# Pooled-key attention with a mixture of adapters on one core: key loads in paced pieces, pooling of later batches on GpSimd, query casts per group, scores four chunks ahead

## The chip, the cores and the metric

The kernel runs on one core of one Trainium2 chip. The metric is device microseconds of a whole execution. Times are medians of repeated executions; the profile is one execution recorded by the hardware profiler, and its span is a little shorter than the device time of the same execution. The engines are PE (TensorE, matmul), PEld (its weight loads), DVE (VectorE), ACT (ScalarE), POOL (GpSimd) and SP (SyncE, which here only issues DMAs). SPq, ACTq and POOLq are the instruction sequencers of those engines.

## The reference

Shapes: `q` is (4, 12288, 128), `kv` is (4, 384, 32, 128), all fp32.

```python
# attention: keys and values are one 4x4 mean pool of kv, projected
kv_pool = kv.reshape(B, H//4, 4, W//4, 4, C).mean(axis=(2, 4))   # 768 keys per batch
k = v = kv_pool.reshape(B, -1, C) @ w_sr
a = softmax(q @ k.T / sqrt(C))
x = (a @ v).reshape(49152, 128)
# mixture of adapters: top 2 of 8 experts by x @ w_gate, softmax over the two
for expert e in the top two:  delta += w_e * (x @ A[e]) @ B[e]     # rank 16
return x + delta
```

## The kernel before

The work is cut into 96 chunks of 512 queries, 24 per batch. Four chunks make a group (`GC = 4`), for which the routing is done at once. The 768 pooled keys of a batch are six key chunks of 128. One pass of the main loop is called a slot. In a slot the kernel computes scores of chunk k, the attention product of chunk k - LA, the normalisation of chunk k - LA - 1, and, later, the adapters of an older chunk. Helpers `keep` and `mm` hold the instructions of each engine in program order.

The key load and its pooling on VectorE:

```python
def load_kv(b, engines):                       # one 6 MB tile for a batch, four DMAs
    t = prep.tile([P, HL, 4, WL * 4, C], FP32, tag="kvr", name="kvr")
    ...
# pool_step, five per third of a batch:
    keep(nc.vector.tensor_tensor(u, u, v, op=ALU.add))
```

The main loop (cut):

```python
LA = 2
for k in range(NCHUNK + LB + 2):
    ...
        if i == 0 and b + 1 < B:
            load_kv(b + 1, [nc.sync])            # 6 MB on the SP queue at once
            cast_q(b + 1, 0, NB // GC)           # q fp32 -> bf16, DRAM to DRAM, whole batch
            pending = prepare(b + 1, 3)
        if k % GC == 0:
            load_qT(k // GC + 2)                 # transposed load, SP queue, two groups ahead
        scores(k, 0)                             # PE sg, ACT exp
    normalize(kn); transposes(kx, kh); ...       # VectorE rinv, xn; PE tt_ps
    top(kn); route(...)                          # VectorE max8, POOL lgs copy, VectorE m, arg, mask, gw
    ...
    finish(kh)                                   # VectorE osb (4 buffers), SP store to out
    ...
    if i >= 3:
        for _ in range(2):
            if pending: pending.pop(0)()         # pooling adds, then key and value projections
```

Three kinds of transfer share the SP queue and pass through it in order: key loads, transposed query loads and output stores. The `lgs` copies, the issues of the query casts and, in the changed kernel, the pooling adds share the GpSimd instruction stream in order. Batches and their keys are counted from 0, as in the code: the keys of batch 2 arrive while batch 1 is computed.

The softmax here doesn't subtract the row's maximum and nothing guards it: scores larger than these inputs give would overflow.

## Time and profile before

| quantity | before | where it is read |
|---|---|---|
| device time, median of 4 runs | 610.21 us (609.62 to 611.39) | timed runs |
| PE busy | 405.8 us, 67% of the span | page, part 1 |
| first score matmul | 76.9 us | timeline of PE |
| steady pace | 3.91 us per chunk (four chunks 15.64) | starts of the normalisation |
| last score to end | 28.2 us (579.8 to 608.0) | timeline of PE |

The page of the kernel before, parts 1 and 2. Part 2 cuts the span in 40 slices, each digit a busy share in tenths; 15 us are one slice.

```profile
PE 405.8 (67%) x4436; PEld 304.1 (50%) x4507; DVE 385.8 (63%) x1045; ACT 289.9 (48%) x313; POOL 23.6 (4%) x107
...
PE   0000270778999920478899970087899999999974
...
DMA  8999099233144999933334699942314444442222
```

PE has no work for four slices at the start, and falls to 0 three times later (slices 7, 16 and 25 to 26), each time where the DMA row is at 9: new keys are arriving.

The waits of the kernel before (who, for what: us in total, times, longest).

```profile
PE acc L66 <- DVE xn L227: 105.9, 30, 31.6
DVE kvr L150 <- DMA kvr<-in_kv_dram: 78.1, 3, 29.3
...
DVE osb L310 <- DMA out_dram<-osb: 7.4, 2, 3.9
```

VectorE runs its instructions in the order of the program. Its first pooling add (`kvr`) of a batch waits for the keys, three times for 78.1 us in total, and everything that VectorE owes to PE waits behind it: PE stands for `xn` as long. The windows show one such stop against a steady stretch (us, then for each engine busy us and instructions, then clock, DMA share and GB/s).

```profile
220.00:240.00 20.00, 0.00 (x0) 0.00 (x0) 0.00 (x0) 0.61 (x1) 0.00 (x0) 0.54 1.03 203
...
480.00:500.00 20.00, 19.72 (x233) 14.90 (x234) 17.43 (x54) 15.74 (x18) 1.06 (x5) 1.00 0.37 94
```

In the first, PE and VectorE do nothing in 20 us while the DMA engines are full at 203 GB/s. In the second, PE is busy 19.72 of 20 us: it is the limit of the steady state. Three groups of the kernel before matter later (busy us, mean ns of one, then idle before).

```profile
L213 ACT ACTIVATE em<-sg 128x1024 f16<-128x1024 f32 x288 | 283.5, 1022 | 231.8 <-PE sg L66 163.7 <-PE d_ps L66 41.2 <-PE acc L66 18.5
...
L150 DVE TENSOR_TENSOR kvr<-kvr 128x1024 f32<-128x1024 f32 (+5 forms) x50 | 54.9, 1113 | 78.6 <-DMA kvr<-in_kv_dram 78.1
...
L265 DVE SCALAR_TENSOR_TENSOR gw<-th,mask 128x128 f32<-128x128 f32 x24 | 6.7, 281 | 0.3 <-ACT th L257 0.3
```

### The profile page before, as it was taken

Reading aid. Unit: us, or ns where it says so; the run is one execution under the profiler, and the core shown is the slowest. Engines: PE = TensorE matmul, PEld = TensorE weight load, DVE = VectorE, ACT = ScalarE, POOL = GpSimd, SP = SyncE. Lnnn points to the kernel's source line nnn. Section 1 sums busy time; section 2 is a strip of 40 time slices with the busy share of each in tenths; the row PEclk is TensorE's granted clock in tenths of the full one; section 3 lists DMA queues with packets and bytes.
Section 4 is the critical chain, followed back from the end, with each engine's and each line's share of the span. In section 5 each row is a group of like instructions: output and inputs, shape, how many; then the busy total and the mean of one; then the engine's idle time right before and its main releaser. Section 6 shows DMA issues by size and latency. Waiting matters only on the chain.

```text
span 608.0 us, 11014 instructions
## 1 busy us (share of the span) xinstructions
PE 405.8 (67%) x4436; PEld 304.1 (50%) x4507; DVE 385.8 (63%) x1045; ACT 289.9 (48%) x313; POOL 23.6 (4%) x107
## 2 busy tenths in 40 slices
PE   0000270778999920478899970087899999999974
PEld 0000140556777710356677750065677777777752
DVE  0002810798788810589788850288878888888884
ACT  0000080455677720146577760054567777777720
POOL 1000000000000000000000000000000000000000
PEclk9999996689999975589999995588999999999995
DMA  8999099233144999933334699942314444442222
GB/s 199 262 250 199 22 205 196 61 71 87 55 105 105 205 193 203 196 61 79 86 90 107 140 203 203 216 104 71 87 53 106 105 105 106 105 106 64 62 80 74
DMA packets 108995, 76.41 MB, mean 126 GB/s; under 512 B 53008, under 2 KB 102416, under 8 KB 108560
## 3 DMA queue, kind: packets, MB, share of 16 engines
q1 hardware_dynamic: 106208, 59.78, 43.3%
q0 software_dynamic: 464, 12.58, 9.9%
q10 hardware_dynamic: 2272, 3.35, 2.3%
q8 instruction: 35, 0.57, 0.4%
q14 instruction: 16, 0.13, 0.1%
HBM read 50.53 MB, written 37.75 MB: 145 GB/s over the span
## 4 chain that ended last, share of the span: by engine, by line
DVE 33%; PE 31%; DMA 26%; SPq 5%; issue 4%; ACT 0%; DVEq 0%; ACTq 0%
DMA kvr<-in_kv_dram 24%; PE acc L66 13%; DVE kvr L150 8%; PE sg L66 7%; DVE xn L227 7%; DVE tts L283 6%; SPq L95 5%; PE d_ps L66 4%; DVE hg L297 4%; PE tt_ps L66 3%; PE h_ps L66 2%; DMA b_f<-in_moe_B_dram 2%; DVE osb L310 2%; DVE rinv L225 2%; DVE gw L265 1%
## 5 line engine op out<-in xcount | busy, mean ns | idle before, releaser
L213 ACT ACTIVATE em<-sg 128x1024 f16<-128x1024 f32 x288 | 283.5, 1022 | 231.8 <-PE sg L66 163.7
L66 PE MATMUL acc<-vx,em 128*128 128x137 f16 x2304 | 181.5, 229 | 107.8 <-DVE xn L227 105.9
L66 PEld LDWEIGHTS <-em 128*128 128x128 f16 x2304 | 155.6, 101 | 140.7 <-DVE xn L227 136.0
L66 PE MATMUL sg<-qT,kfT 128*128 128x512 bf16 x505 | 158.6, 385 | 2.6 <-ACT em L213 2.3
L150 DVE TENSOR_TENSOR kvr<-kvr 128x1024 f32<-128x1024 f32 (+5 forms) x50 | 54.9, 1113 | 78.6 <-DMA kvr<-in_kv_dram 78.1
L310 DVE TENSOR_TENSOR osb<-d_ps,xn 128x512 f32<-128x512 f32 x96 | 66.2, 690 | 25.1 <-PE d_ps L66 17.8
L66 PEld LDWEIGHTS <-tts 128*128 128x128 bf16 x768 | 53.2, 101 | 45.7 <-DVE tts L283 22.9
L227 DVE TENSOR_TENSOR xn<-acc,rinv 128x544 f32<-128x544 f32 x96 | 69.5, 724 | 3.3
L297 DVE TENSOR_TENSOR hg<-h_ps,gw 128x512 bf16<-128x512 f32 x96 | 66.3, 691 | 5.4 <-PE h_ps L66 2.9
L283 DVE COPY tts<-tt_ps 128x1024 bf16<-128x1024 bf16 (+1 forms) x97 | 65.9, 680 | 2.6 <-PE tt_ps L66 2.6
L66 PEld LDWEIGHTS <-kfT 128*128 128x128 bf16 x576 | 46.7, 99 | 7.7 <-issue 5.4
L66 PE MATMUL d_ps<-b_bf,tts 128*128 128x128 bf16 x384 | 39.6, 228 | 6.3 <-DVE tts L283 4.1
L66 PEld LDWEIGHTS <-xn 128*128 128x128 bf16 x384 | 29.7, 98 | 28.0 <-issue 7.1
L66 PE MATMUL tt_ps<-id_bf,xn 128*128 128x128 bf16 x384 | 37.5, 221 | 7.1 <-DVE osb L310 5.9
L241 POOL COPY lgs<-xn 128x32 f32<-128x32 f32 x96 | 20.3, 211 | 563.9 <-DVE xn L227 563.9
L66 PE MATMUL h_ps<-a_bf,tts 128*128 128x128 bf16 x384 | 39.1, 227 | 1.5 <-issue 0.4
L66 PE MATMUL tt_ps<-id_bf,hg 128*128 128x128 bf16 x384 | 38.0, 222 | 2.0 <-DVE hg L297 2.0
L66 PE MATMUL wT_ps<-id_f,w_sr_sb 128*128 128x128 f32 x1 | 0.4, 448 | 56.9 <-DMA w_sr_sb<-in_w_sr_dram 56.9
L225 DVE RECIPROCAL rinv<-acc 128x4 f32<-128x4 f32 x96 | 17.1, 178 | 29.9 <-PE acc L66 29.7
L240 DVE MAX8 srt<-xn 128x8 f32<-128x8 f32 x384 | 34.7, 152 | 0.1
L120 DVE COPY wext<-w_sr_sb 128x128 f32<-128x128 f32 x1 | 0.2, 227 | 54.1 <-DMA w_sr_sb<-in_w_sr_dram 54.1
L66 PEld LDWEIGHTS wT_ps<-id_f,w_sr_sb 128*128 128x128 f32 x1 | 0.2, 183 | 56.9 <-issue 56.9
(81 smaller groups left out, 109.3 us busy)
## 6 DMA issues: line engine op xcount, KB each, us to landing
out_dram<-osb SPq DMA_DIRECT2D x96, 256.0 KB, 2.3
kvr<-in_kv_dram SPq DMA_DIRECT2D x14, 1536.0 KB, 31.8
kvr<-in_kv_dram ACTq DMA_DIRECT2D x2, 1536.0 KB, 49.7
qbf_0_174<-in_q_dram POOLq DMA_DIRECT2D x1, 3072.0 KB, 38.5
qbf_0_1807<-in_q_dram POOLq DMA_DIRECT2D x1, 3072.0 KB, 18.5
qbf_0_3695<-in_q_dram POOLq DMA_DIRECT2D x1, 3072.0 KB, 19.3
qbf_1_165<-in_q_dram POOLq DMA_DIRECT2D x1, 2560.0 KB, 22.9
qbf_0_98<-in_q_dram POOLq DMA_DIRECT2D x1, 512.0 KB, 10.0
```

The costliest lines, as they stand in the source:

```text
L66: return keep(nc.tensor.matmul(*a, **k))
L95: keep(engines[w % len(engines)].dma_start(t[32 * w:32 * w + 32].rearrange("p l r x c -> p l r (x c)"), src[w]))
L150: keep(nc.vector.tensor_tensor(u, u, v, op=ALU.add))
L213: keep(nc.scalar.activation(em[k][:, 2 * r:2 * r + 2], ps, AF.Exp, bias=0.0, scale=scale))
L225: keep(nc.vector.reciprocal(ri, acc[k][:, :, VC]))
L227: keep(nc.vector.tensor_tensor(x, acc[k][:, :, 0:VC], ri.unsqueeze(2).broadcast_to([P, S, VC]), op=ALU.mult))
L240: keep(nc.vector.max(srt[g][:, m, s], xn[k][:, s, C:VC]))
L241: keep(nc.gpsimd.tensor_copy(lgs[g][:, m], xn[k][:, :, C:VC]))
L265: keep(nc.vector.scalar_tensor_tensor(w, th, 1.0, mask, op0=ALU.add, op1=ALU.mult))
L283: keep(nc.vector.tensor_copy(sb[:, lo:hi], ps[:, lo:hi]))
L297: keep(nc.vector.tensor_tensor(hg[k].rearrange("p s (e r) -> p (s e) r", e=E), hp[k].rearrange("p s (e r) -> p (s e) r", e=E), gw[g][:, m ...
L310: keep(nc.vector.tensor_tensor(osb, dp[k], xn[k][:, :, 0:C], op=ALU.add))
```

## The change

The intent: start the matmuls while the first keys still arrive, keep the waiting for later keys off VectorE, and take the pooling work (54.9 us of VectorE) away from it for three of four batches. The diff, cut to its core:

```diff
-    qpool bufs=3, ppool bufs=3, xpool bufs=12                  # (shortened)
+    kvpool bufs=4, qpool bufs=4, ppool bufs=7, xpool bufs=9    # opool stays at 4
@@ start
-    load_kv(0, [nc.sync, nc.scalar])
-    cast_q(0, 0, 1)
+    cast_q(0)                                   # a cast is now one group, not a batch
+    for g in range(J):                          # six 1 MB pieces, each four DMAs
+        load_kv(0, g // WL, slice(4 * (g % WL), 4 * (g % WL) + 4), [nc.sync, nc.scalar])
+        if g == 2:
+            load_qT(0)
@@ first group
+    for h in range(3):                          # pool and project two key chunks,
+        for item in sums[10 * h:10 * h + 10] + rest[2 * h:2 * h + 2]:
+            item()
+        for k in range(LA):                     # then their scores for four query chunks
+            scores(k, h)
@@ scores
-    ... AF.Exp, bias=0.0, scale=scale)
+    ... AF.Exp, bias=shift, scale=scale)        # shift: a tile of -0.25
@@ main loop
-    LA = 2
+    LA = 4
-        load_kv(b + 1, [nc.sync]); cast_q(b + 1, 0, NB // GC); pending = prepare(b + 1, 3)
-        load_qT(k // GC + 2)
+            if g + 1 < B * NG and g + 1 not in qT:
+                load_qT(g + 1)                  # one group ahead
+            if g + 2 < B * NG and g + 2 not in q_bf:
+                cast_q(g + 2)
+            if i == 4:
+                sums, rest = prepare(b + 1, nc.gpsimd)
+            if i in (4, 5, 6):                  # 2 MB pieces, three slots in a row
+                load_kv(b + 1, i - 4, slice(0, 2 * 4), [nc.sync])
+            if i >= 8:                          # three pooling adds per slot
+                for _ in range(3):
+                    if sums: sums.pop(0)()
@@ end of a slot
+        if i >= 18 and rest:                    # projections of the next batch's keys
+            rest.pop(0)()
+            if len(rest) > NB - 1 - i:
+                rest.pop(0)()
@@ routing groups
+    sizes = [GC] * (NCHUNK // GC - 2) + [2, 2, 2, 1, 1]
```

## The prediction

> **What bounds it now.** Three regimes. (a) Start: the windows show no matmul work until 57 us; the timeline has the first score matmul at 76.9 us after 13 us of serial VectorE pooling. (b) Steady state (windows 460 to 580): PE busy 19.7 of every 20 us, 3.91 us per chunk (acc chain, 15.63 us per four chunks). (c) Batch changes: the chain of waits has "DMA kvr" at 24% of the span. VectorE's in-order pooling waits for the next keys, so everything stops, about 20 us at 87 to 107, 32 at 216 to 248 and 31 at 360 to 392 (waits: DVE kvr <- DMA 78.1 us in three waits). Then pooling (54.9 us over four batches) makes VectorE the limit, about 5.2 us per chunk for some ten chunks.
>
> **What the change does.**
> 1. Start: pooling per 1 MB piece and the scores of four chunks overlap the load; weights go first. From the DMA packets: keys 31 us of all engines, three casts about 3.2 us each, one transposed load 2.7. I expect keys to end near 46 us, first scores at 20 to 25, the main loop near 53. Saves about 25 us.
> 2. Pooling of batches 1 to 3 goes to GpSimd. The Trainium skill, "GPSIMD Engine Reference", section 3.1, has a two-input fp32 add at 4497 ns for 2048 elements; so I estimate 1.2 us for 128x512, 0.65 and 0.35 for the small ones, 28 us per batch, at most 3.7 us per chunk, just under 3.91. "SBUF — State Buffer", section "SBUF: two separate sides", lets GpSimd block VectorE only in two-SBUF-input or 2-port operations; the large VectorE ones here read PSUM (xn 724, osb 690, hg 691 ns should stay). VectorE then needs 3.4 us per chunk; PE bounds. Saves about 31 us.
> 3. The stalls: VectorE no longer waits for keys. But output stores and transposed query loads share the SP queue, first in first out, behind 6.3 MB of keys (30 us at 204 GB/s measured), plus casts, which take nearly all engines when active (packets). With four output buffers, stores behind the second and third key piece land late: I expect VectorE (osb <- DMA out_dram) or PE (sg <- DMA qT, now prefetched one group ahead, not two) to stall 10 to 20 us per batch, about 45 in all, instead of 84.
> 4. Tail: smaller last routing groups, about 5 to 8 us less than the 28 after the last score.
>
> **Sum.** 53 start + 92 iterations x 3.91 = 360, less 5 for the empty first ones, + 14 for key/value projections on PE + 20 tail = 442, if nothing stalls; + 45 = 487. I shade to 483, as the placement looks tuned against such stalls. Nearly all is on the critical path. Range 452 to 512; faster 0.98, same 0.01, slower 0.01.
>
> **What would show it.** Step 1: first sg before 27 us, PE dense from about 53. Step 2: POOL kvr groups near 1.2 us at 128x512, POOL busy about 105 us, no DVE kvr after 50 us. Step 3: the waits list "DVE kvr <- DMA" gone from batch changes; in its place one idle stretch of 10 to 20 us per batch around slots 8 to 12, ended by out_dram or qT.
>
> **What would make it wrong.** Stores not stuck behind keys (then 440 to 450); GpSimd adds at 1.7 us or more, so that its in-order lgs copies hold up routing (then above 500); VectorE lengthened by GpSimd; 2 KB key packets slower than 4 KB ones, delaying the start.

## The result and the profile after

| | median us | fast runs, lowest to highest | ratio to before, 95% interval |
|---|---|---|---|
| before | 610.21 | 609.62 to 611.39 | |
| after | 513.12 | 510.90 to 515.95 | 0.841 (0.836 to 0.846) |

A ratio, here and below, is the mean time of one kernel's fast runs over that of the other's fast runs of the same rounds, so it is not quite the ratio of the medians. The change is worth 16%. All outputs are right. The prediction had 483 us with a range that ended at 512; the measured median lies just above that range.

The page of the kernel after, parts 1 and 2; a slice is now 12.8 us.

```profile
PE 411.9 (80%) x4444; PEld 302.6 (59%) x4515; DVE 362.4 (71%) x1048; ACT 313.2 (61%) x316; POOL 121.9 (24%) x216
...
PE   0025799899999954798999967589899999999973
...
DMA  9999999464464999954645899956446566552222
```

PE is dense from the sixth slice on, but two dips, to 4 and to 5, remain, where the DMA row again is at 9. The waits name what is waited for now.

```profile
PE tt_ps L67 <- DVE osb L304: 24.7, 10, 5.9
DVE osb L304 <- DMA out_dram<-osb: 23.4, 4, 7.5
...
DVE arg L247 <- POOL lgs L237: 9.8, 2, 5.5
...
PE sg L67 <- DMA qT<-qbf_100: 6.4, 1, 6.4
```

VectorE no longer waits for keys at a batch change: its `kvr` line is down to 14.6 us in four waits, all in the first 40 us. It waits for its own output buffers: `osb` needs one of four buffers, and the store that empties it has not landed (23.4 us in four waits). PE's next transposes (`tt_ps`) wait for VectorE as long. VectorE also waits twice for the `lgs` copy of GpSimd, which stands behind a pooling add whose keys have not arrived. The chain of waits of the kernel after has the first stall in three pieces (start us, us, what).

```profile
171.30 17.93 DMA kvr<-in_kv_dram
189.29 15.92 DMA out_dram<-osb
205.31 0.70 DVE osb L304
```

The store issued at 189.29 landed at 205.21. Twelve key DMAs of 512 KB, issued from 167.9 to 187.2, landed one after the other until 204.8. The stores took their place among them: the one issued at 170.00 landed at 182.08, the one issued at 176.20 at 194.71. The median store takes 2.7 us from issue to landing. The Trainium skill, "DMA: Bandwidth & Descriptors", section "Queues, rings and completion order", says that each DMA engine consumes a queue's descriptors in ring order; these landing times agree. The trace shows a second thing about this queue: the DMAs of SP and ScalarE count their landing on eight semaphores in turn, and an issue waits until the DMA that used its semaphore before has landed. The store of 189.29 had been written by VectorE at about 187.2, and was issued 0.06 us after a key load had landed at 189.23; so large loads also hold back the issue of what comes behind them. No run separates this from the order of the queue. The timeline of VectorE (start, us, then the idle time before) shows the same stall from its side.

```profile
185.62 0.79 DVE L247 SCALAR_TENSOR_TENSOR arg<-lgs,m_2439 128x128 f32<-128x128 f32 x1 [5.50 <-POOL lgs L237]
...
187.13 1.17 DVE L259 SCALAR_TENSOR_TENSOR gw<-th,mask 128x128 f32<-128x128 f32 x1
...
194.80 0.69 DVE L304 TENSOR_TENSOR osb<-d_ps,xn 128x512 f32<-128x512 f32 x1 [3.98 <-DMA out_dram<-osb]
...
205.31 0.69 DVE L304 TENSOR_TENSOR osb<-d_ps,xn 128x512 f32<-128x512 f32 x1 [7.49 <-DMA out_dram<-osb]
```

The windows of the kernel after give the size: from 180 to 220 us PE was busy 23.9 of 40 us. The last line, from the end of the run, has VectorE at 18.5 of 20 us and PE at 15.8: in the tail VectorE is the fuller engine.

```profile
160.00:180.00 20.00, 19.77 (x236) 15.08 (x237) 16.99 (x55) 16.45 (x18) 1.62 (x6) 1.00 0.90 179
180.00:200.00 20.00, 11.64 (x118) 8.44 (x118) 8.16 (x22) 8.55 (x9) 12.81 (x15) 0.83 1.06 233
200.00:220.00 20.00, 12.25 (x127) 8.90 (x128) 12.87 (x33) 9.50 (x10) 9.32 (x14) 0.91 1.01 195
480.00:500.00 20.00, 15.79 (x219) 13.11 (x216) 18.51 (x61) 3.74 (x5) 1.06 (x5) 1.00 0.31 89
```

Groups of the kernel after, kept apart by shape:

```profile
L202 ACT ACTIVATE em<-sg,shift 128x1024 f16<-128x1024 f32 x288 | 306.8, 1111 | 112.1 <-PE sg L67 67.8 <-PE acc L67 14.9 <-PE tt_ps L67 12.8
...
L259 DVE SCALAR_TENSOR_TENSOR gw<-th,mask 128x128 f32<-128x128 f32 x22 | 9.4, 426 | 0.2 <-ACT th L251 0.2
...
L146 POOL TENSOR_TENSOR kvr<-kvr 128x512 f32<-128x512 f32 x54 | 68.5, 1279 | 11.2 <-DMA kvr<-in_kv_dram 5.7 <-PE d_ps L67 4.5
...
L146 POOL TENSOR_TENSOR kvr<-kvr 128x256 f32<-128x256 f32 x18 | 13.1, 726 | 0.9
L146 POOL TENSOR_TENSOR kvr<-kvr 128x128 f32<-128x128 f32 x18 | 9.0, 502 | 1.0
```

The GpSimd adds took 1279, 726 and 502 ns. The large VectorE operations kept their durations (`xn` 724 to 725, `osb` 690 to 689, `hg` 691 to 691 ns), but the small routing operation `gw` rose from 281 to 426 ns in the mean. The exponential rose from 1022 to 1111 ns. The edit to it is that its bias is now a tile: the Trainium skill, "ScalarE: Activation LUTs", in the section "What ACT_TABLE_LOAD costs", gives about 93 ns for each such operand, and the 89 ns measured here agree. ScalarE is not the limit, so this cost nothing that the trace shows.

### Where the time went, chunk by chunk

The start of the normalisation (`xn`) of every chunk gives the time per chunk. In a quiet stretch four chunks take 4.17 + 3.81 + 3.83 + 3.83 = 15.64 us. Against this the profiled execution after shows:

- The main loop starts at about 60.4 us, and the first normalisation at 64.3.
- The fifth to eighth chunk of batches 1 and 2 (chunks 28 to 31 and 52 to 55), where the keys of batches 2 and 3 arrive, take 10.95, 7.00, 10.50 and 4.43 us, and 9.74, 8.06, 9.87 and 5.72. That is 17.2 and 17.8 us above 15.64. While the keys of batch 1 arrive, there is no such stall. These 35.0 us are close to VectorE's waits for `out_dram` and for `lgs` together (23.4 + 9.8).
- Chunks 14 to 19 of each of the first three batches, where the projections of the next keys run, take 5.60, 5.57, 4.47, 4.62, 5.04 and 5.04: 6.9 us above six quiet chunks, three times.
- Two routing chunks of each of these batches take 6.00 and 5.09 in place of 4.17 us: 2.75 us more, three times. The first of them in VectorE's timeline:

```profile
91.95 0.60 DVE L245 TENSOR_TENSOR m_831<-srt 128x16 f32<-128x16 f32 x1
...
92.66 1.23 DVE L247 SCALAR_TENSOR_TENSOR arg<-lgs,m_831 128x128 f32<-128x128 f32 x1
...
94.62 0.76 DVE L259 SCALAR_TENSOR_TENSOR gw<-th,mask 128x128 f32<-128x128 f32 x1
```

- The last score matmul ends at about 482.4 us, and the end is at 512.7: a tail of 30.3 us.

### The profile page after: what moved, and what is told of

Its sections match the earlier page's. It is cut to its first block, busy times and chain, and to the rows that moved or that the text cites. A ratio compares the mean times of both kernels' runs of the same rounds, so it can differ in the third digit from the quotient of the medians.

```text
span 512.7 us, 11238 instructions
## 1 busy us (share of the span) xinstructions
PE 411.9 (80%) x4444; PEld 302.6 (59%) x4515; DVE 362.4 (71%) x1048; ACT 313.2 (61%) x316; POOL 121.9 (24%) x216
## 4 chain that ended last, share of the span: by engine, by line
PE 39%; DVE 30%; DMA 18%; issue 7%; SPq 2%; POOL 2%; ACT 1%; DVEq 0%; POOLq 0%
PE acc L67 16%; DMA kvr<-in_kv_dram 11%; PE sg L67 9%; DVE xn L216 7%; DVE tts L277 6%; DMA out_dram<-osb 6%; PE d_ps L67 5%; PE tt_ps L67 4%; DVE hg L291 3%; PE h_ps L67 3%; DVE rinv L214 2%; DVE gw L259 2%; POOL kvr L146 1%; DMA b_f<-in_moe_B_dram 1%; SPq L83 1%
## 5 line engine op out<-in xcount | busy, mean ns | idle before, releaser
L202 ACT ACTIVATE em<-sg,shift 128x1024 f16<-128x1024 f32 x288 | 306.8, 1111 | 112.1 <-PE sg L67 67.8
L67 PE MATMUL acc<-vx,em 128*128 128x137 f16 x2304 | 178.0, 226 | 6.7 <-DVE xn L216 4.3
L67 PEld LDWEIGHTS <-em 128*128 128x128 f16 x2304 | 152.8, 99 | 39.3 <-DVE xn L216 32.4
L67 PE MATMUL sg<-qT,kfT 128*128 128x512 bf16 x505 | 162.2, 394 | 15.4 <-ACT em L202 7.5
L304 DVE TENSOR_TENSOR osb<-d_ps,xn 128x512 f32<-128x512 f32 x96 | 66.1, 689 | 38.8 <-DMA out_dram<-osb 23.4
L146 POOL TENSOR_TENSOR kvr<-kvr 128x512 f32<-128x512 f32 (+2 forms) x90 | 90.1, 1013 | 13.1 <-DMA kvr<-in_kv_dram 5.7
L67 PEld LDWEIGHTS <-tts 128*128 128x128 bf16 x768 | 52.6, 100 | 41.6 <-DVE tts L277 18.5
L67 PEld LDWEIGHTS <-kfT 128*128 128x128 bf16 x576 | 47.7, 100 | 26.4 <-issue 20.4
L67 PE MATMUL h_ps<-a_bf,tts 128*128 128x128 bf16 x384 | 37.6, 221 | 1.3
L67 PEld LDWEIGHTS <-hg 128*128 128x128 bf16 x384 | 25.0, 99 | 13.1 <-DVE hg L291 12.7
L251 ACT ACTIVATE th<-arg 128x128 f32<-128x128 f32 (+2 forms) x27 | 8.0, 298 | 39.6 <-DVE arg L247 30.4
L146 DVE TENSOR_TENSOR kvr<-kvr 128x512 f32<-128x512 f32 (+2 forms) x30 | 16.1, 556 | 15.3 <-DMA kvr<-in_kv_dram 14.6
```

What stands on the lines that cost most here:

```text
L67: return keep(nc.tensor.matmul(*a, **k))
L146: keep(adder.tensor_tensor(u, u, v, op=ALU.add))
L202: keep(nc.scalar.activation(em[k][:, 2 * r:2 * r + 2], ps, AF.Exp, bias=shift, scale=scale))
L251: keep(nc.scalar.activation(th, arg, AF.Tanh, bias=0.0, scale=0.5))
L304: keep(nc.vector.tensor_tensor(osb, dp[k], xn[k][:, :, 0:C], op=ALU.add))
```

## The experiments

The theory after the comparison: (A) the stalls while the keys of batches 2 and 3 arrive come from stores, and transposed query loads, that queue behind 6 MB of keys issued in three successive slots; (B) projections and routing blocked by GpSimd make a part of the loop slower; (C) the tail and the start were mis-sized. The rivals: the number of output buffers alone is the fault; the start itself is what costs; GpSimd pooling costs more than it saves. Every experiment is an edit of the kernel after, and each was timed beside the kernel before on its chip. Kernels of one call share a chip: first the four directly below (in the expectations e1, e2, e3 and e8), then the two with another queue for the keys, the projections and the routing groups (e4 to e7), then the early queries, the later casts and the first combination (e9 to e11), then the last alone (e12).

### More output buffers

```diff
-    opool = ctx.enter_context(tc.tile_pool(name="opool", bufs=4))
+    opool = ctx.enter_context(tc.tile_pool(name="opool", bufs=12))
```

> Only change to the changed kernel: 12 output buffers in place of 4. Theory F (stores and query loads sit behind 6.3 MB of keys in one first-in-first-out queue): the waits of VectorE for out_dram (23.4 us in four) vanish, but PE then waits at slot 12 for the transposed query load that is behind the same keys (it landed at 207.8 us while its scores were only due at about 210 because of the stall), so little is won: 2 to 6 us in all, 508 to 511 us. Rival theory B (four output buffers are the fault by themselves): the 23 us go, 490 us. Rival theory G (GpSimd's in-order lgs copies behind late keys are what stalls): nothing changes.

Two of four runs were slow, the profiled one too. The fast ones took 524.41 and 527.89 us, ratio 0.862 (0.857 to 0.867): slower than the kernel after, not faster. The waits of this profile have no line for `out_dram` any more, but this one:

```profile
PE sg L67 <- DMA qT<-qbf: 34.8, 3, 16.4
```

PE now waits for the queries of the next group. Their transposed load, behind the keys in the same queue, was issued from 200.12 to 211.17 us and landed at 225.80; a query cast in flight at the same time, issued at 206.57, landed at 225.59. Since that profile is of a slow execution, its durations are not compared with others. That this wait is what made the fast runs slow is argued from it, and the next experiment tests it. The rival "the buffers alone" falls.

### More output buffers, queries two groups ahead

```diff
 (opool bufs=12 as above)
-            if g + 1 < B * NG and g + 1 not in qT:
-                load_qT(g + 1)
-            if g + 2 < B * NG and g + 2 not in q_bf:
-                cast_q(g + 2)
+            if g + 2 < B * NG and g + 2 not in qT:
+                load_qT(g + 2)
+            if g + 3 < B * NG and g + 3 not in q_bf:
+                cast_q(g + 3)
```

(With one more cast and one more transposed load before the loop.)

> 12 output buffers, and query loads (and casts) issued two groups ahead, so before the keys in the queue. Theory F: both victims of the queue are relieved, the stalls of batches 2 and 3 fall from about 17.5 us to the 5.5 us that routing waits for lgs; 20 to 27 us less, 486 to 493 us. Theory B: no better than with the buffers alone. Theory D (the DMA engines are simply full in that stretch and the loss moves elsewhere): within 6 us of 513.

Measured: 502.84 us (499.79 to 504.43), ratio 0.823 (0.819 to 0.827). It is 22 to 25 us faster than the fast runs with more buffers alone, and 10 us faster than the kernel after. The waits of its fast profile:

```profile
PE sg L67 <- DMA qT<-qbf: 8.0, 2, 4.2
```

There is no `out_dram` line, and the query wait is short. So the queries were indeed the next thing to be late. Their load was still slow: issued from 198.63 to 214.51, landed at 227.87, with a cast in flight that landed at 227.67. The gain is half of the expected 20 to 27 us, and the trace accounts for it: the two stalls shrank to 8.1 and 7.3 us, 19.7 less, but the one cast and load more before the loop go with a first normalisation 4.2 us later (68.5), and chunk 36 took 9.1 in place of 5.1 us. VectorE still waited 10.2 us in two waits for the `lgs` copies.

### Key pieces four slots apart

```diff
-            if i in (4, 5, 6):
-                load_kv(b + 1, i - 4, slice(0, 2 * 4), [nc.sync])
+            when = (4, 5, 6) if b == 0 else (0, 4, 8)
+            if i in when:
+                load_kv(b + 1, when.index(i), slice(0, 2 * 4), [nc.sync])
```

> Four output buffers and prefetch of one group as in the changed kernel; only the three key pieces of batches 2 and 3 are issued in slots 0, 4 and 8 in place of 4, 5 and 6 (batch 1 as before). Same bytes, same queue. Theory F: no more than one 2 MB piece (10 us) is ever in front of a store or a query load, less than the 15.6 us that four buffers or one group give: stalls of batches 2 and 3 fall from 17.5 us to under 3 us each, so about 30 us less, 480 to 486 us, and the lgs wait goes as well because the first piece is there before slot 8. Theory D: the time stays near 510.

Measured: 491.80 us (490.08 to 494.15), ratio 0.805 (0.801 to 0.809), 21.3 us faster than the kernel after. This leaves the number of buffers and the prefetch as they were and changes only when the keys are issued. Its waits and its windows:

```profile
DVE osb L304 <- DMA out_dram<-osb: 5.1, 2, 3.2
...
PE sg L67 <- DMA qT<-qbf: 1.7, 1, 1.7
```

```profile
170.00:190.00 20.00, 16.32 (x180) 12.42 (x180) 15.13 (x41) 12.85 (x13) 9.23 (x13) 0.93 1.08 231
190.00:210.00 20.00, 18.19 (x212) 13.77 (x215) 16.76 (x44) 14.11 (x15) 14.33 (x19) 0.99 1.04 223
```

From 170 to 210 us PE was busy 34.5 us, with as many bytes on the move as in the stall of the kernel after. Chunks 28 to 31 took 7.98, 5.03, 3.84 and 3.84 us, 5.1 us above quiet; chunks 52 to 55 took 6.0 above. Theory (A) holds: when the keys are issued in the shared queue makes 21 us. The edit does two things at once, though: the pieces are further apart, and the first comes four slots earlier. The two waits for `lgs` (9.8 us) are gone as well, and how much of the 21 us each of the two makes is not separated here. The gain is smaller than the expected 30, as about 11 us of stall are left.

### Pooling back on VectorE

```diff
-                sums, rest = prepare(b + 1, nc.gpsimd)
+                sums, rest = prepare(b + 1, nc.vector)
```

> Undo one part: pooling of batches 1 to 3 on VectorE again, all else as changed. Theory: three batches of 13.4 us of VectorE adds (30 at 69 percent of the GpSimd time or less), in slots 8 to 17 where VectorE has only about 0.5 us per slot free, so 8 to 10 us per batch, plus some more of the wait for late keys: 25 to 35 us slower than changed, 538 to 548 us. Rival (the gain of the change comes from the placement of the loads alone, the engine of the pooling does not matter): within 6 us of 513.

Measured: 533.79 us (529.20 to 534.97), ratio 0.873 (0.869 to 0.878), 20.7 us slower than the kernel after. The expected size was 25 to 35 us. In this kernel VectorE waits 26.8 us for keys, in six waits that include those of the start, and the pooling chunks take 4.6 to 5.1 us. With GpSimd idle in those slots, `gw` is back at its old duration:

```profile
L259 DVE SCALAR_TENSOR_TENSOR gw<-th,mask 128x128 f32<-128x128 f32 x22 | 6.2, 282 | 0.5 <-ACT th L251 0.5
```

So the move to GpSimd is worth 20.7 us net, although it lengthens the routing. This is work and waiting together: the same edit raises VectorE's wait for keys from 14.6 to 26.8 us. The rival "GpSimd costs more than it saves" falls.

### The start: which queue brings what

Three kernels ask whether an earlier start brings time. In the kernel after, ScalarE's sequencer needed 35.5 us to issue its half of the first keys, and the first transposed query load was late; the timeline of the kernel after (start, us):

```profile
1.66 35.54 ACTq L94 DMA_DIRECT2D kvr<-in_kv_dram  x12
...
16.49 6.66 SPq L83 DMA_TRANSPOSE qT<-qbf_100  x1
...
35.00 1.86 PE L67 MATMUL sg<-qT,kfT 128*128 128x512 bf16 x4 [6.40 <-DMA qT<-qbf_100]
...
42.09 4.34 ACT L202 ACTIVATE em<-sg,shift 128x1024 f16<-128x1024 f32 x4
```

The scores were there from 35.0 us on, but ScalarE's first exponential ran at 42.1, after its last DMA issue (until 40.7) and a table load of 1.28 us. The twelve issues themselves took 4.2 of the 35.5 us. In the rest ScalarE waited for semaphores: each of the last eight key issues came 0.02 us after the landing of the DMA that had used its semaphore before (28.18 after 28.16, 33.53 after 33.51). First, the half of ScalarE goes to the GpSimd queue, once behind three casts and once with the later casts behind the keys:

```diff
-        load_kv(0, g // WL, ..., [nc.sync, nc.scalar])
+        load_kv(0, g // WL, ..., [nc.sync, nc.gpsimd])
     # e4: identity and casts 0 to 2 before the keys on GpSimd;  e5: cast 0 before, casts 1 and 2 after
```

> Start only. In the changed kernel ScalarE issues half of the first batch's key loads and its sequencer is held by them for 35.5 us, so its first exp comes at 42.1 us although scores were due at 29 and the first queries landed near 35; PE, in order behind two full score tiles, and VectorE behind PE then wait. Here GpSimd's queue takes ScalarE's half (behind the same first three casts, so the bytes and their order are nearly the same). Theory S (ScalarE held as issuer): first exp near 36 us, main loop (first normalise, 64.3 us before) 4 to 7 us earlier, 506 to 509 us in all. Rival K (arrival of the last keys, near 46 us, sets the start): first exp earlier, but first normalise within 2 us of 64.3, time 511 to 514.

> As e4, but only the first group's cast goes before the keys; the other casts stand behind them in GpSimd's queue. In the changed kernel the casts took nearly all DMA engines from about 5 to 14 us and the keys had a fifth of them. If the arrival of keys counts (K, or both S and K), keys end 6 to 9 us earlier and the first normalise comes at 50 to 56 us; 500 to 505 us in all. If only S counts: as e4.

Measured: 511.92 us (511.20 to 514.41), ratio 0.840, with the casts first, and 515.26 (513.37 to 517.21), ratio 0.845, with them last. Neither differs from the kernel after (0.841) by more than the intervals allow, and neither start came as expected: theory S had 4 to 7 us for e4, where 2.3 came, and e5 was to have its first normalisation at 50 to 56. The first exponential came earlier in e4 (37.2 in place of 42.1 us), but the transposed load was issued from 9.6 to 31.8 us and landed at 36.1, and the keys behind it on SP waited: first normalisation at 62.0. In e5 the query load landed only at 42.5, and the first normalisation came at 68.0.

The third puts the queries early: the transposed load goes behind the first piece, all keys on SP, and casts 1 and 2 are held back on GpSimd by tiny copies that read a landed piece.

```diff
-        load_kv(0, g // WL, ..., [nc.sync, nc.scalar])
-        if g == 2:
+        load_kv(0, g // WL, ..., [nc.sync])
+        if g == 0:
             load_qT(0)
...
     for g in range(1, 3):
+        keep(nc.gpsimd.tensor_copy(hold[:, g - 1:g], kvr[0, g][:, 0, 4, 0:1]))
         cast_q(g)
```

> Start, third theory. In the changed kernel and in e4 and e5 the first transposed query load stands in the middle of the SP queue's keys and took 18.5 (issue 16.5, landed 35.0), 26.5 and 32.5 us, while keys or casts of another queue were in flight; the SP half of the last three pieces was only issued behind it. Theory X: that load, not ScalarE's issuing and not the order of casts, sets the start. Here it is issued behind the first 1 MB piece alone, all keys go on SP, and the casts of groups 1 and 2 are held back until the pieces before them have landed. X expects the first queries landed by 14 us, first scores by 26, last keys by 43 to 45, first normalise at 54 to 58 us (64.3 in the changed kernel), 503 to 507 us in all. If only the total of bytes counts, first normalise stays at 62 to 65 and the time at 511 to 514.

Measured: 516.67 us (512.88 to 517.64), ratio 0.846 (0.842 to 0.851): no gain, although the start became better in every reading. The query load was issued at 9.62 and landed at 13.98, the first scores ran at 25.2, the last keys landed at 40.2, and the first normalisation came at 56.4, 7.9 us earlier than in the kernel after. The gain was given back in chunk 8, which took 16.1 us in place of 6.0. The waits name it:

```profile
PE sg L67 <- DMA qT<-qbf: 10.9, 1, 10.9
```

The queries of the fourth group were issued at 67.66 us, behind the 6 MB of batch 1's keys (landed until 85.3), and landed at 93.85, with a cast issued at 80.31 that landed at 93.66. An earlier loop only reached the queue of the next keys earlier. The start alone is not worth anything until batch 1 is paced too.

### Projections over more slots

```diff
-        if i >= 18 and rest:
-            rest.pop(0)()
-            if len(rest) > NB - 1 - i:
-                rest.pop(0)()
+        if i >= 16 and rest:
+            rest.pop(0)()
```

> Key and value projections of batches 1 to 3 one item per slot from slot 16, in place of two items in slots 18 and 19. Slots with a transposition and the projection behind it in a row took 5.6 us against 3.83, slots with one of them 0.3 and 0.8 us over. Theory L (in these slots PE stands behind VectorE's copy of the transposed keys): 0.6 us less in each of two slots per batch, 3 to 5 us less in all, 508 to 510 us. Rival W (it is the fp32 matmul work itself): unchanged within 1.5 us.

Measured: 510.31 us in five runs (508.86 to 511.52), ratio 0.837 (0.834 to 0.840), 2.8 us less than the kernel after, with intervals that overlap. The trace agrees in size: chunks 12 to 19 took 38.2 in place of 39.2 us, and with the same gain in each of three batches that makes 3 us. A part of the 20.6 us of projections is bunching; the larger part stayed.

### No small routing groups at the end

```diff
-    sizes = [GC] * (NCHUNK // GC - 2) + [2, 2, 2, 1, 1]
+    sizes = [GC] * (NCHUNK // GC)
```

> Undo the small last routing groups (all groups of four chunks). The prediction gave them 5 to 8 us of the tail; the profile has 30.3 us from the last score to the end against 28 before the change, though with four chunks outstanding in place of two. Theory T (they do save, and the four outstanding chunks cost it again): 4 to 8 us slower without them, 517 to 521 us. Rival (VectorE-bound tail, the split brings nothing): within 2 us of 513.

Measured: 518.49 us in six runs (515.03 to 520.62), ratio 0.850 (0.847 to 0.854): 5.4 us slower. So the small groups do what they were predicted to do (5 to 8 us). The long tail has another cause.

### More output buffers, with the casts two slots later

```diff
 (opool bufs=12)
-            if g + 2 < B * NG and g + 2 not in q_bf:
-                cast_q(g + 2)
+        if k % GC == 2 or k == LA:
+            g = k // GC
+            if g + 2 < B * NG and g + 2 not in q_bf:
+                cast_q(g + 2)
```

> e1 (12 output buffers) came out slower than the changed kernel, with PE waiting 16 us for a transposed query load that was in flight together with a cast (206.6 to 225.6) and stores. Here casts are issued two slots later in each group, so that the cast of slot 12 does not meet the late query load of slot 8; otherwise as e1. Theory X (a transposed load and a cast in flight together hold each other up): the wait of PE for qT falls from some 17 us to under 8 us per batch, 505 to 513 us. If e1's wait is only the queue of keys in front of the load: unchanged, 522 to 530 us.

Measured: 502.85 us (501.82 to 504.41), ratio 0.825 (0.823 to 0.827). It differs from the first experiment only in when a cast is issued, and is 22 to 25 us faster than that one's fast runs. Its fast profile:

```profile
PE sg L67 <- DMA qT<-qbf: 11.2, 3, 5.4
```

The query load was issued from 189.99 to 203.16 and landed at 205.22; the cast beside it (188.76 to 200.12) had landed before the issue was over. That is the difference between the two traces, of which the first is of a slow execution. Over the traces of the changed kernel and of all experiments, a transposed load landed 2.1 to 2.3 us (medians) after the end of its issue when no cast was in flight at that moment. In 19 loads one was in flight; 16 of them landed only after that cast, and seven within 0.25 us of it: 225.80 after 225.59, 227.87 after 227.67, 93.85 after 93.66, and four more. These seven took 4.9 to 14.6 us from the end of the issue. These numbers alone show little: five of the 16 landed the usual 2.0 to 2.2 us after the end of their issue, and without a cast the first load of the kernel after took 11.8 us, among the keys. But the same traces have the pair with no keys in flight. In the kernel after, a cast and a load are issued in the same slot; in this one the cast comes two slots later (first the kernel after, then this one):

```profile
210.35 6.16 SPq L83 DMA_TRANSPOSE qT<-qbf_2398  x1
```

```profile
338.50 2.49 SPq L83 DMA_TRANSPOSE qT<-qbf  x1
```

In the kernel after, 15 loads without keys had a cast beside them: their issue took 4.5 to 6.6 us (median 5.4), and they landed 7.9 us after its start. Here 16 loads had neither: 2.0 to 4.1 us (median 2.3), landed after 4.6. The number of buffers is not the reason: the kernel with 12 buffers and queries two groups ahead, which has the cast in the same slot, had a median of 5.3. So a cast beside a transposed load costs the load about 3 us, and moving the casts away goes with 22 us less among the keys. Why the two hinder each other stays open, and so does how much of the 22 us is this effect: moving a cast also changes what the keys share the engines with.

### Everything that helped, together

The combination has the early queries, the pieces at slots 0, 4 and 8 for batches 2 and 3, projections from slot 16, eight output buffers, and casts three groups ahead at the third slot of a group. The second kernel also paces batch 1:

```diff
-            when = (4, 5, 6) if b == 0 else (0, 4, 8)
+            when = (4, 7, 10) if b == 0 else (0, 4, 8)
...
-            if i >= 8:
+            if i >= (9 if b == 0 else 8):
                 for _ in range(3):
```

> Meant as a better version: the start of e9, keys of batches 2 and 3 in slots 0, 4 and 8 (e3), projections spread (e6), eight output buffers, casts of group g+3 in the middle of a group. If the gains add (8 to 10 us start, 21 pacing, 3 spread), 475 to 484 us; if pacing and start share their gain, about 490.

> e9 brought the first normalise to 56.4 us (64.3 in the changed kernel) and still won nothing: its chunk 8 took 16.1 us in place of 6.0, for the query load of group 3, queued behind all keys of batch 1, landed at 93.9. If that queue is what took the gain back (theory F once more), spreading batch 1's three key pieces too (slots 4, 7 and 10 in place of 4, 5 and 6, pooling from slot 9), on top of e11, brings chunk 8 back to some 6 us: 467 to 471 us against e11's 478. If the DMA engines are simply full until then, the loss moves to another slot and the time stays within 3 us of 478.

Measured: 478.01 us (477.09 to 479.80), ratio 0.784 (0.782 to 0.787), and 472.73 us (471.25 to 473.32), ratio 0.774 (0.772 to 0.776). The second is the fastest kernel of this study: 40.4 us faster than the kernel after and 137.5 faster than the kernel before. In the first, chunk 8 still took 14.2 us with a query wait of 7.6 us; in the second it took 5.1, chunks 28 to 31 took 5.52, 3.81, 3.83 and 3.84, and its list of waits has no line for `out_dram` and none for `qT`. Its window at the place of the old stall:

```profile
180.00:200.00 20.00, 18.39 (x214) 13.52 (x212) 17.05 (x48) 14.72 (x16) 15.71 (x21) 1.00 1.09 228
```

PE is busy 18.4 of 20 us with 228 GB/s moving. It ended 2 us above its expected range of 467 to 471.

## Why the prediction was wrong in size

The direction and most mechanisms were right: a saving of 97 us was measured where 127 was predicted. What failed are costs in its sum. Step 2 let GpSimd's adds leave VectorE's routing alone (0 us; measured 8.2). Step 4 took the small last groups off the old tail without the two more chunks that `LA = 4` leaves to it (20 us; measured 30.3). Step 1 and the term for the projections were too short (53 us, measured 60.4; 14, measured 20.6). The prediction was a sum, and the profiled execution gives each term:

| term | predicted us | measured us | difference |
|---|---|---|---|
| start until the main loop | 53 | 60.4 | +7.4 |
| 92 slots at 3.91 | 360 | 360 | 0 |
| first, half-empty slots | -5 | about -1.5 (the remainder: it makes the sum come out) | +3.5 |
| projections | 14 | 20.6 | +6.6 |
| routing held up by GpSimd | 0 | 8.2 | +8.2 |
| stalls at batch changes | 45 | 35.0 | -10.0 |
| tail after the last score | 20 | 30.3 | +10.3 |
| shading for tuning | -4 | 0 | +4 |
| sum | 483 | 513 | +30 |

Point by point:

- **The stalls (right in mechanism, too large by 10 us).** The prediction said that stores behind the second and third key piece land late, that VectorE would stall on `osb`, 10 to 20 us per batch, and that "DVE kvr <- DMA" would vanish from the batch changes. All of this is in the trace: 17.2 and 17.8 us. Only the keys of batch 1 came without a stall. A part was not foreseen: 9.8 of the 35.0 us are VectorE waiting for `lgs` copies behind a pooling add on GpSimd. The prediction feared this only for adds of 1.7 us or more; the adds took 1.28, and it was late keys that held them. The pacing experiment showed that the issue pattern is the cause: it took 21.3 us away by moving issue slots alone.
- **The start (mis-sized by 7.4 us).** First scores "at 20 to 25" came at 35.0, because the transposed load took from 16.49 to 34.96 us behind keys, and the exponentials had to wait for ScalarE's DMA issues until 42.1. Keys ended at 47.7, close to the predicted 46. When an experiment made the predicted start (first scores at 25.2), the time did not improve: the step "Saves about 25 us" ("Nearly all is on the critical path") failed in that a better start first needs the next keys out of the way. In the last kernel, with both, the first normalisation at 55.6 us is kept.
- **GpSimd's effect on VectorE (the dismissed term, 8.2 us).** The prediction named the rule of the Trainium skill, "SBUF — State Buffer", section "SBUF: two separate sides", that a VectorE operation with two inputs in SBUF can be blocked by GpSimd, and then looked at the large operations only. These did stay at 725, 689 and 691 ns. But `m`, `arg` and `gw` have both inputs in SBUF. In the slot at 92 us they took 0.60, 1.23 and 0.76 us in place of 0.19, 0.29 and 0.28, which is 1.83 us, and this chunk took 6.00 in place of 4.17 us. (`mask` has both inputs in SBUF too; it kept 0.28 us here and took 0.38 in the mean of the kernel with paced keys, so it is not always the same operations that are hit.) With the pooling back on VectorE, `gw` had 282 ns again. The trace agrees with the page; the prediction read past it, though it named "VectorE lengthened by GpSimd" among what would make it wrong.
- **GpSimd's own cost (a good estimate).** Predicted 1.2, 0.65 and 0.35 us from the 4497 ns that "GPSIMD Engine Reference", section 3.1, gives for 2048 elements; measured 1.28, 0.73 and 0.50. A pure scaling misses a fixed part: the three sizes lie near 240 ns plus 2.0 ns per element. POOL was busy 121.9 us, predicted about 105.
- **The gain of the move (about a third too large).** Predicted 31 us; undoing it cost 20.7, and this includes the longer wait for keys.
- **Projections (6.6 us).** The term counted PE time; the slots took more, because VectorE's copies out of PSUM and the pairing of two items in one slot are on the way as well. Spreading them gained 2.8 us, so the bunching is seen in the trace, though the intervals of the times overlap, and the rest is argued.
- **The tail (10.3 us).** The small last groups gained 5.4 us, as predicted. The prediction took this off the old 28 us and left out what the same diff does with `LA = 4`: at the last score, four chunks in place of two still have their attention product and their normalisation to come. Two chunks at about 4.5 us, what chunks 90 to 95 took on average (26.65 us for six), are about 9 us. This is an estimate from the trace; `LA` itself was not varied. The kernel without small groups fits it: its tail is 36.6 us, 8.4 more than the 28.2 of the kernel before, which also has none.
- **The shading (4 us).** "The placement looks tuned against such stalls" was an assumption. Slots 4, 5 and 6 are not tuned: 0, 4 and 8 were 21 us better at the first try.

No single term explains the miss. Six under-sized terms of 3.5 to 10.3 us pointed the same way, and the only over-sized one gave 10 us back; that the total is off by no more than 30 us is in part this luck.

## What to carry to other kernels

When loads, stores and prefetches share one queue, the distance in time between large loads is a parameter of its own: issue them no faster than the loop can wait for the small transfers behind them, and check every kind of transfer in that queue, since freeing one only shows the next. When work moves to GpSimd, list every VectorE operation with two SBUF inputs, the small ones too, and count how often each comes due while GpSimd works. A saving in the start is only time saved if the next shared resource is free earlier as well; look at where the loop runs into its next wait before counting it.

## What the Trainium skill lacked or had wrong

- The time that a transposed load loses beside a casting DMA (page "DMA: Bandwidth & Descriptors", whose X-bar section warns of two transposing streams only). With no keys in flight, loads with a cast beside them took a median of 7.9 us from the start of the issue to landing, loads without one 4.6.
- How long one transposed load holds the sequencer that issues it (same page, section "Issuing engines are not separate DMA queues", which calls the time to initiate a DMA usually small). The plain DMAs of the kernel after agree (a median of 0.37 us), but its transposed loads held SP for 1.6 to 19.3 us, with a median of 5.6.
- The cost of completion semaphores that are used again (no page has it). Here the DMAs of SP and ScalarE shared eight; ScalarE needed 35.5 us for twelve issues of 4.2 us in all, and its first exponential waited.
- A fixed cost in ns for a GpSimd elementwise operation ("GPSIMD Engine Reference", section 3.1, has a two-input add at one size only). Measured adds of 512, 256 and 128 elements: 1279, 726 and 502 ns.
- The durations behind the VectorE slowdown under GpSimd work ("SBUF — State Buffer", section "Who interferes with whom", has the rule and a factor, but no size of the operations). Here an operation of 0.29 us took up to 1.23 us beside GpSimd adds of 1.28 us.
